# Reordering the seven first-layer products of a chunk: 1 2 6 5 7 1' 3 instead of 1 2 5 6 1' 3 7

## The chip, the cores and the metric

The kernel runs on one core of a Trainium2 chip. The metric is the device time of one launch in microseconds (us), the median of three runs. Engines are named as in the profile: PE is the matmul engine, PEld its weight loads, DVE the vector engine, ACT the scalar engine, POOL the GpSimd engine, SP the engine that issues most of the DMAs. Results of matmuls land in PSUM[...]; ACT and DVE read them from there.

## The reference

Two blocks follow each other. The first is an attention with a threshold, over 8 batches, 8 heads, 576 positions and a head width of 64, and the second a two-layer network on its output as 4608 tokens of width 512:

```python
def _attn_ref(q, k, v, tau) -> np.ndarray:
    scale = 1.0 / np.sqrt(q.shape[-1])
    scores = scale * np.matmul(q, k.transpose(0, 1, 3, 2))
    thresh = np.max(scores, axis=-1, keepdims=True) - tau
    scores = np.where(scores >= thresh, scores, -1000000000.0)
    scores = scores - np.max(scores, axis=-1, keepdims=True)
    attn = np.exp(scores)
    attn = attn / (np.sum(attn, axis=-1, keepdims=True) + 1e-09)
    return np.matmul(attn, v).astype(np.float32)

def _moe_ref(x, w_in, w_out) -> np.ndarray:
    h = x @ w_in
    r = np.maximum(h, 0.0)
    g = r * r
    return (g @ w_out).astype(np.float32)
```

`w_in` is 512 x 2048 and `w_out` 2048 x 512. All is in float32.

## The kernel before

The kernel interleaves the two blocks on one core. Attention runs in steps: a step takes 128 query rows of a pair of heads. The network runs in 18 chunks of 256 tokens, numbered 0 to 17. A chunk is cut into pieces (a handful of matmuls each), and the pieces are put between the attention's instructions as filler for PE: `fill` and `piece` take them from a queue in order, by a fixed count of microseconds per piece, not by a clock. So the place of each instruction in its engine's queue is set when the program is built[...].

**First layer of chunks 2 to 17.** These chunks compute x @ w_in as a 2 x 2 block product with seven block products instead of eight, on sums and differences of the blocks of x and of w_in. Each product comes in two halves of the hidden width; the first half is written "1", the second "1'". So there are 14 units, and `UNITS` gives their order. A unit (`unit`, line 678) is eight matmuls of 128 x 128 x 128 (line 693), 16 rows in the profile, since each float32 matmul shows as two. Its result needs a PSUM bank of 512 columns. The units build on each other in place:

- Product 1 takes a bank. Once it has been copied out, product 6 adds to the same bank; once 1+6 has been copied out, product 7 adds to it; once that has been read, product 4 adds.
- Product 5 takes a bank; once it has been copied out, product 3 adds to it.
- Product 2 takes a bank of its own.

In that stage the units have three banks (5, 6 and 7), so 1' takes the bank that product 2 leaves, and 2' the one that product 3 leaves.

**The readers of the banks.** After a unit, `then` (line 708) reads its bank into the buffer `g`: a copy on ACT for products 1 (line 713), 6 (line 718), 5 (line 725) and 7' (line 729), an add on DVE for 2, 3, 7, 2', 3' and 5' (line 705), and for 4 and 4' the activation itself. After an add, ACT runs the activation, Relu and Square (lines 701 and 702). `then` is issued one piece after its unit and the activation one piece after that (`after`, line 946), or earlier where an attention step calls `after` between pieces. On ACT these copies and activations stand in one queue with the attention's: two small ones (lines 340 and 341), two exponents (line 343) and a copy of one column (line 309) that makes ACT wait for the scores. On DVE the adds stand with the maxima of the scores (line 317), the threshold with its sum (line 355), the small lines 359 and 360, the turning of blocks (lines 459 to 469 and 254), and some sums of weight blocks (line 624).

**What else the units use.** The sums of token blocks T1, T2 (tile `t`), T3 (in place in `xT`) and T4 (in `held`) are made by POOL at line 670; unit 5 uses T1, 6 uses T2, 7 uses T3, 4 uses T4. The sums of weight blocks for 6, 5 and 3 are made at line 624, on POOL or, for 6' and 3', on DVE; they lie in `g`, in `gsum` and in `turned`, and some of them are made only when an earlier unit's `then` has asked for them.

**Around it.** The attention's scores are line 296 on PE, its values (weights times v) line 530, whose weights come by DMA through a store aside in DRAM (`aside`). POOL divides the weights (lines 365 and 367). The second layer (line 799) is again a seven-product form, in 14 pieces per chunk; its product 1 is put before the units 3' and 4'. The last three chunks run after the attention has ended, so nothing of it stands between their units.

The lines that carry the dependence on banks:

```python
        if p in "125":
            used[p, q] = keep_bank((p, q))
        to = used[{"6": "1", "7": "1", "4": "1", "3": "5"}.get(p, p), q].rearrange("p (f n) -> p f n", f=4)
```

## Time and profile before

| what | value |
|---|---|
| time, median of 3 runs | 1320.76 us (1320.71 to 1320.98) |
| the profiled execution's own time | 1320.85 us |
| its span in the profile | 1319.1 us |
| mean granted TensorE clock | 0.997 |
| line 693 (units), PE | 3584 rows, 272 to 377 ns each, median 275 |
| line 705 (adds), DVE | 96 of 680 ns median |
| line 713, copy of product 1 in chunk 6, ACT | 0.59 us |
| idle of DVE before line 705, waiting for line 693 | 78.1 us, 33 times |
| idle of ACT before line 713, waiting for line 693 | 39.7 us, 13 times |

A page of the profile shows one execution: the busy time of each engine, the span in 40 slices, the chain of work that ended last, and groups of instructions with the idle time of their engine before them. The timeline gives the instructions of a window in order, with start and length in us; instructions of one kind that follow each other are merged, so that "x32" at line 693 is two units. The arrow in brackets names what ended an engine's idle time. The ends of matmuls are modelled, so that a unit seems to end some 0.16 us after the next has begun.

### The profile page before, as it was taken

How to read it: one execution, taken by the hardware profiler on the slowest of the kernel's cores; microseconds unless marked ns; L12 is line 12 of the kernel's file. 1: busy time of each engine (PE TensorE's matmuls, PEld its weight loads, DVE VectorE, ACT ScalarE, POOL GpSimd, SP SyncE). 2: the span in 40 equal slices, each digit the busy share in tenths (PEclk: the TensorE clock that was granted, in tenths of full speed). 3: DMA queues.
4: the chain of work that ended last, by engine and by line, in shares of the span. 5: the costliest groups of instructions: out<-in, count | busy, mean ns of one | idle time of the engine just before them, and what ended most of it. 6: DMA issues, size and time to landing. Idle time of an engine off the chain costs nothing.

```text
span 1319.1 us, 24730 instructions
## 1 busy us (share of the span) xinstructions
PE 1290.9 (98%) x8862; PEld 1070.6 (81%) x8862; DVE 936.9 (71%) x2034; ACT 585.4 (44%) x1353; POOL 776.2 (59%) x908
## 2 busy tenths in 40 slices
PE   7999999999999999999999999999999999999997
PEld 6676557897888888797978888888887988889997
DVE  6899776777777788788776877878686877522131
ACT  4887763244343526253435343525353434331331
POOL 3788874775747475556574746656574737455351
PEclk9999999999999999999999999999999999999999
DMA  6765431777777878686666768667676866520000
GB/s 127 156 181 145 126 73 60 145 173 168 165 173 178 181 177 186 143 200 160 170 157 158 158 154 187 172 137 185 146 173 139 198 162 161 144 53 9 9 17 17
DMA packets 320907, 185.48 MB, mean 141 GB/s; under 512 B 282224, under 2 KB 282256, under 8 KB 314384
## 3 DMA queue, kind: packets, MB, share of 16 engines
q1 hardware_dynamic: 309120, 115.78, 46.4%
q0 software_dynamic: 10000, 67.92, 12.9%
q8 instruction: 70, 1.15, 0.4%
q14 instruction: 53, 0.43, 0.1%
q10 hardware_dynamic: 1664, 0.21, 0.1%
HBM read 108.04 MB, written 68.42 MB: 134 GB/s over the span
## 4 chain that ended last, share of the span: by engine, by line
PE 83%; DVE 6%; DMA 3%; ACT 2%; issue 1%; POOL 1%; SPq 0%; DVEq 0%; POOLq 0%; ACTq 0%
PE big L693 29%; PE big L799 28%; PE big L530 10%; PE big L296 8%; PE big L579 3%; PE big L764 2%; PE big L280 2%; DVE st L317 1%; DMA wT<-aside 1%; DMA aside<-turned 1%; PE big L414 1%; DVE w L355 1%; ACT w L343 1%; DVE turned L154 0%; PE big L273 0%
## 5 line engine op out<-in xcount | busy, mean ns | idle before, releaser
L355 DVE SCALAR_TENSOR_TENSOR w<-big,st,w 128x576 f32<-128x576 f32 x269 | 207.4, 805 | 87.6 <-ACT w L343 85.6
L317 DVE TENSOR_REDUCE st<-big 128x1 f32<-128x576 f32 x288 | 204.1, 747 | 85.3 <-PE big L296 60.6
L367 POOL TENSOR_SCALAR w<-w,st 128x576 f32<-128x576 f32 x269 | 244.2, 916 | 29.4 <-DVE st L360 24.6
L799 PE MATMUL big<-wo,gsum 128*128 128x256 f32 x1088 | 243.8, 382 | 0.0
L799 PEld LDWEIGHTS big<-wo,gsum 128*128 128x128 f32 x1088 | 204.4, 190 | 37.0 <-issue 7.6
L693 PE MATMUL big<-xT,w_in_sb 128*128 128x128 f32 x1536 | 187.4, 277 | 1.5 <-DVE g L705 1.4
L693 PEld LDWEIGHTS big<-xT,w_in_sb 128*128 128x128 f32 x1536 | 178.5, 192 | 10.8 <-issue 7.7
L799 PE MATMUL big<-wo,g 128*128 128x256 f32 x816 | 185.3, 382 | 0.1
L343 ACT ACTIVATE w<-big,st 128x576 f32<-128x576 f32 x255 | 174.4, 735 | 0.2 <-issue 0.2
L799 PEld LDWEIGHTS big<-wo,g 128*128 128x128 f32 x816 | 151.6, 190 | 26.2 <-issue 6.5
L530 PE MATMUL big<-wT,vs 128*64 128x256 f32 (+5 forms) x1420 | 159.5, 389 | 4.9 <-DMA wT<-aside 3.5
L530 PEld LDWEIGHTS big<-wT,vs 128*64 128x64 f32 (+1 forms) x1420 | 86.0, 136 | 70.1 <-issue 20.8
L340 ACT ACTIVATE st<-st 128x2 f32<-128x2 f32 (+1 forms) x137 | 28.1, 205 | 253.3 <-DVE st L317 252.1
L365 POOL TENSOR_SCALAR st<-st 128x2 f32<-128x2 f32 (+1 forms) x148 | 35.6, 241 | 177.7 <-DVE w L355 167.1
L436 POOL DMA_DIRECT2D aside<-turned x50 | 29.9, 597 | 177.5 <-DVE turned L465 177.5
L705 DVE TENSOR_TENSOR g<-big,g 128x512 f32<-128x512 f32 x96 | 64.6, 676 | 83.7 <-PE big L693 78.1
L296 PE MATMUL big<-kT,qT 64*128 64x256 f32 (+3 forms) x768 | 107.0, 416 | 0.0
L296 PEld LDWEIGHTS big<-kT,qT 64*128 64x128 f32 x768 | 84.6, 186 | 14.5 <-issue 5.0
L701 ACT ACTIVATE g<-g 128x512 f32<-128x512 f32 x96 | 60.4, 630 | 63.5 <-DVE g L705 63.4
L569 POOL TENSOR_TENSOR gsum<-g 128x512 f32<-128x512 f32 x34 | 46.1, 1356 | 69.9 <-ACT g L702 69.6
L702 ACT ACTIVATE g<-g 128x512 f32<-128x512 f32 x128 | 80.9, 632 | 4.0
L459 DVE STREAM_TRANSPOSE turned<-w 128x512 f32<-128x512 f32 x100 | 70.2, 702 | 0.3 <-issue 0.3
(119 smaller groups left out, 2058.1 us busy)
## 6 DMA issues: line engine op xcount, KB each, us to landing
aside<-turned POOLq DMA_DIRECT2D x50, 1152.0 KB, 4.8
wT<-aside SPq DMA_DIRECT2D x200, 288.0 KB, 5.4
vs<-in_v_dram SPq DMA_DIRECT2D x72, 128.0 KB, 5.7
wo<-in_moe_w_in_dram SPq DMA_DIRECT2D x16, 512.0 KB, 4.8
wo<-in_moe_w_out_dram SPq DMA_DIRECT2D x16, 512.0 KB, 3.5
out_dram<-osb POOLq DMA_DIRECT2D x32, 256.0 KB, 3.9
kl<-in_k_dram SPq DMA_DIRECT2D x113, 72.0 KB, 2.8
ql<-in_q_dram SPq DMA_DIRECT2D x112, 72.0 KB, 5.7
```

The lines of the kernel that those rows point to most:

```text
L296: nc.tensor.matmul(big[to, at + x0:at + x1], lhsT, keys[u * D:(u + 1) * D, x0:x1], start=True, stop=True)
L317: nc.vector.tensor_reduce(out=mx[:, u:u + 1], in_=sc[u], axis=AX.XY, op=ALU.max)
L343: nc.scalar.activation(out=w[:, u, :].rearrange("p (h k) -> p h k", h=2), in_=sc[u], func=AF.Exp, bias=bias[:, u:u + 1], scale=SCALE)
L355: nc.vector.scalar_tensor_tensor(out=wu, in0=sc[u], scalar=thr[:, u:u + 1], in1=wu, op0=ALU.is_ge, op1=ALU.mult, accum_out=sm[:, u:u + 1])
L367: nc.gpsimd.tensor_scalar(out=w[:, u, :], in0=w[:, u, :], scalar1=z[:, u:u + 1], scalar2=rcp[:, u:u + 1], op0=ALU.add, op1=ALU.mult)
L459: move(wb[:, 0:h, :, :], whole_[:, 0, :, :, :])
L530: nc.tensor.matmul(ps[u * D:(u + 1) * D, :], vs[n % 2][rows, u * (NBLK + 1) + c, :], wT[rows, at // REST:(at + ps.shape[1]) // REST, NBLK ...
L693: nc.tensor.matmul(to[:, f, :], factor(j, p, q, c)[:, f * P:(f + 1) * P], part[:, c, :], start=(p in "125" and f == 0 and c == 0), stop=(p ...
L701: nc.scalar.activation(out=to, in_=to if src is None else src, func=AF.Relu)
L702: nc.scalar.activation(out=to, in_=to, func=AF.Square)
L705: nc.vector.tensor_tensor(out=x, in0=to, in1=x, op=ALU.add)
L799: nc.tensor.matmul(to, left[:, f, :], wo[:, slot, f, :], start=(f == 0), stop=(f == HF - 1))
```

## The change

One string is changed, the order of the first twelve units. Products 6 and 5 change places, 7 moves from behind 3 to before 1', and 1' and 3 move back by one. From 6' on the order is as it was, and so are the two units that follow product 1 of the second layer.

```diff
-    UNITS = [(p[0], len(p) - 1) for p in "1 2 5 6 1' 3 7 6' 2' 4 7' 5'".split()], [("3", 1), ("4", 1)]
+    UNITS = [(p[0], len(p) - 1) for p in "1 2 6 5 7 1' 3 6' 2' 4 7' 5'".split()], [("3", 1), ("4", 1)]
```

The readers and requests that hang on a unit move with it: its copy or add, its activation, and the sums that its `then` asks for. It holds for chunks 2 to 17; chunks 0 and 1 don't use `UNITS`.

## The prediction

> **What bounds the kernel now.** I read the page first: its part on busy time, the 40 slices, then the chain that ended last.

> ```profile
> PE 1290.9 (98%) x8862; PEld 1070.6 (81%) x8862; DVE 936.9 (71%) x2034; ACT 585.4 (44%) x1353; POOL 776.2 (59%) x908
> ...
> PE   7999999999999999999999999999999999999997
> ...
> PE 83%; DVE 6%; DMA 3%; ACT 2%; issue 1%; POOL 1%; SPq 0%; DVEq 0%; POOLq 0%; ACTq 0%
> ```

> PE is busy 98% of the span, in every slice but the first and last at nine tenths or more, and the chain is PE for 83%. No other engine passes 71%. So a microsecond in which PE newly waits is a microsecond of time, and one that PE no longer waits comes off. What the other engines do counts only where PE waits for it.

> Next I asked for the instructions of line 693 (the units), and what ended PE's idle time before them:

> ```profile
>   issue: 12.9, 36
>   DVE g L705: 3.7, 6
>   POOL g L624: 1.7, 2
>   POOL gsum L624: 0.3, 1
>   POOL gsum L569: 0.3, 1
>   ACT g L718: 0.3, 1
> ```

> Real waits before 1,792 unit matmuls are 6.3 us in all (everything but "issue"). That is the most this stage can give back. The order of before costs nearly nothing, so what matters is whether the new order adds waits. The timeline of PE, ACT and DVE around chunk 6 (columns: start, length, engine, line, operation, operands, count, and idle time before it) shows how close the readers of the banks are:

> ```profile
> 558.32 3.84 PE L693 MATMUL big<-xT,w_in_sb 128*128 128x128 f32 x32
> ...
> 561.07 0.59 ACT L713 COPY g<-big 128x512 f32<-128x512 f32 x1
> ...
> 561.99 3.74 PE L693 MATMUL big<-t,g 128*128 128x128 f32 x32
> ...
> 564.75 0.68 DVE L705 TENSOR_TENSOR g<-big,g 128x512 f32<-128x512 f32 x1
> ...
> 565.46 0.63 ACT L701 ACTIVATE g<-g 128x512 f32<-128x512 f32 x1 [3.80 <-DVE g L705]
> 565.57 1.97 PE L693 MATMUL big<-xT,w_in_sb 128*128 128x128 f32 x16
> 566.12 0.63 ACT L702 ACTIVATE g<-g 128x512 f32<-128x512 f32 x1
> 566.66 0.57 ACT L725 COPY g<-big 128x512 f32<-128x512 f32 x1
> 567.13 0.59 ACT L718 COPY g<-big 128x512 f32<-128x512 f32 x1
> ```

> Units 1 and 2 run from 558.32, units 5 and 6 from 561.99, unit 1' from 565.57: a unit takes 1.79 us of PE. Unit 1's bank is copied at 561.07, unit 6's at 567.13, though unit 6 ended at 565.73: ACT stood at L701, which waited 3.80 us for DVE's add of unit 2. What a wait for a bank looks like is shown in chunk 12, where 1' takes the bank of unit 2 (read by DVE until 968.76):

> ```profile
> 968.82 2.05 PE L693 MATMUL big<-xT,w_in_sb 128*128 128x128 f32 x16 [0.96 <-DVE g L705]
> ```

> PE starts 0.06 us after the read ends, and this unit takes 1.89 instead of 1.79 us: 0.1 us a restart. The same 0.06 is in chunk 4 (423.38, 423.43).

> [...] the copy of unit 6 above stands behind L701. [...] the waits below stay under 2 us, so I cost no clock. The trace of before agrees in so far as its waits of 0.4 to 1 us at lines 530 and 693 left the granted clock at 9 tenths or more in every slice.

> **The change part by part.** Matmuls, copies, adds, squares and SP's DMAs are the same in number and size; SP's order is the same. The pieces keep their 14 places; only what stands in places 3 to 7 changes: 5 6 1' 3 7 becomes 6 5 7 1' 3. Banks stay: 1, 6, 7, 4 share one, 5 and 3 another, 1' takes that of 2, and 2' that of 3. The distances from a read to the unit that needs it done become:

> - 6 after the copy of 1 (L713): units between fall from two to one
> - 7 after the copy of 6 (L718): from two to one
> - 6' after the copy of 1': from two to one
> - 2' after the add of 3 (L705): from two to one
> - 3 after the copy of 5 (L725): two, as before
> - 1' after the add of 2: from two to three; 4 after the add of 7: from two to four

> One unit between leaves about 1.6 us from the end of the unit to the end of its read. With an empty ACT a copy ends 0.62 us after its unit (last three chunks of the trace), so these chunks, without attention beside them, lose nothing. In the others ACT's queue decides. In the new order of ACT's instructions the copy of 6 stands where that of 5 stood or earlier, so I take the time of the instruction in that slot from the timeline. Chunk by chunk, in us:

> - chunk 2: slot of copy 6 is that of L725, ended 282.69; unit 7 was due at 282.14: 0.61. Then 1' stands behind a group of scores (L296), and its copy behind that step's two exponents (L343, ended 288.95, now 0.6 later) and behind L701 and L702: 289.6+0.6+0.6+0.6=291.4; 6' was due at 290.5: 0.9. With two restarts 1.7.
> - chunk 5: L725's slot ended 495.33; place 5 began at 493.58: 1.8.
> - chunk 6: 567.23 against 565.57: 1.7, restart 0.1: 1.8.
> - chunk 8: 698.56 against 697.79: 0.8, restart 0.1: 0.9.
> - chunk 9: 767.07 against 765.87: 1.26 and 0.1. Unit 3 now stands behind the scores, and its add behind DVE's L317, L469, L355, L359, L360, which ended at 776.02 and come 1.4 later; with 0.65 for the add, 778.1; 2' is due at 776.7: 1.5 and 0.1. Together 2.95.
> - chunk 10: copy of 1 ended 827.41, unit 6 is due at 825.81: 1.66 and 0.1: 1.75.
> - chunk 11: copy of 1 ended 895.15, due 893.25: 1.96 and 0.1; unit 5's wait for POOL's L624 there (0.73 in the trace, its place 1.03 too long) goes: 1.0.
> - chunk 12: copy of 1 ended 965.70, due 964.04: 1.7 and 0.1; copy of 6 in the slot ending 970.56, so place 5 begins at 970.62 instead of 968.82, the wait of 1' included: 1.8 in all.
> - chunk 13: copy of 1' behind L355, L360 (ended 1042.2), add of 7, L701, L702: about 1044.7; 6' due at 1044.05: 0.75 and 0.1; a wait of 0.3 before 7' goes: 0.5.
> - chunk 4: the wait of 1' (0.44) goes, 3 waits for the copy of 5, which now stands behind the exponents (L718's slot, ended 426.89) as long: -0.1.
> - chunks 3, 7, 14: reads end 0.3 to 1 us early: nothing. Chunks 15 to 17: nothing.

> Sum: 1.7+1.8+1.8+0.9+2.95+1.75+1.0+1.8+0.5-0.1 = 14.1 us.

> Moved on DVE: the add of 7 now stands ahead of L317 or L355 of an attention step, so that step's maxima or threshold come up to 3 us later (chunk 8: unit 7 ends about 700.7, L317 began at 698.37). Behind them wait the exponents, POOL's division, the turning and the store aside. The steps' values are multiplied three or four steps later, so I cost nothing; without that cover L530 would wait, as it did for 3.5 us in all on DMA before. A later PE may shorten that 3.5: 0 to -2. Moved on POOL: in five chunks (3, 4, 10, 13, 14) the two sums for 5' (L624, 1.3 us each) go behind a division; chunk 4 is tightest, done at about 437 with 5' due at 438.4: nothing. T3 was done 10 us or more before its first use in most chunks and 5 us in chunk 15: nothing.

> The profiled execution took 1320.85 us, with 1319.1 of span and 1.75 around it; the median is 1320.76, so the two are one for this purpose. 1320.85+14.1 = 1335.0.

> **Rivals.**
> - Half of it: PE's delay and shifts in DVE's queue spare several of the waits, and only those from ACT's slots just behind exponents hold (5, 6, 10, 12: 7.2 us, less 2 for DMA waits): 1326. For it: DVE's L624 took 0.67 to 2.18 us, and the add of 2 behind it moves with it. Against: a unit and its copy shift together.
> - Cascade: the late adds on DVE and copies on ACT reach the tight places (chunks 4, 7, 11, 14, each with 0.1 to 1 us left) and L530's transfers: 8 us more, 1343.
> - Faster: the longer distances for 1' (add of 2), 4 and 5 remove the waits of the L693 view, of which 3.7 us are DVE's and 2.0 POOL's L624, while the copy of 6 gets ahead of L701 everywhere as it does in chunks 3, 4, 13 and 14. Then 1320.85-3 = 1318. It decides if the copies of 1 and 6 end within 1.6 us of their units; the slots above speak against it in eight chunks.
> - Nothing: gains and losses of 2 us each: 1320.8. It needs the same early copies.

> **How the numbers follow.** Forecast 0.70 (own range 1330 to 1340), half 0.14, cascade 0.09, faster 0.03, nothing 0.04. The range 1326 to 1342 leaves out the two last cases, half of the half and part of the cascade. A measurement of this kernel tells about 0.2%, 2.6 us, from no change: faster 0.03, same 0.05, slower 0.92.

> **What would show it.** Idle of PE before L693 ended by ACT's L713 and L718 should appear with some 10 to 12 us, by DVE's L705 some 1.5 to 3. In chunk 6 the fifth unit should start 1.7 us after the fourth ended. The last three chunks should be as long as before. PE's busy time should stay. If the L693 view shows no ACT release, the forecast is wrong; if L530 waits for DMA far more than 3.5 us, it is the cascade.

## The result and the profile after

| what | before | after |
|---|---|---|
| time, median of 4 runs each, same chip | 1320.74 us (1319.98 to 1320.98) | 1335.74 us (1333.27 to 1338.4) |
| ratio, 95% interval | | 1.0115 (1.0095 to 1.0135) |
| the profiled execution: time, span | 1320.85, 1319.1 us | 1335.76, 1334.0 us |

The new order costs 15 us. The page of after, its parts on busy time and on the chain that ended last:

```profile
PE 1294.1 (97%) x8862; PEld 1071.7 (80%) x8862; DVE 937.6 (70%) x2034; ACT 583.4 (44%) x1353; POOL 776.3 (58%) x908
...
PE 79%; DVE 8%; ACT 3%; DMA 3%; issue 2%; POOL 0%; SPq 0%; DVEq 0%; ACTq 0%; POOLq 0%
```

The counts of instructions are those of before, and PE is still what bounds the kernel. Its busy time grew by only 3.2 us, the span by 14.9: the rest is idle time of PE. What ended the idle time before line 693 (us, times; rows of PE and of weight loads together):

```profile
  issue: 14.0, 38
  ACT g L718: 13.7, 12
  ACT g L713: 7.7, 7
  POOL gsum L624: 3.9, 3
  DVE g L705: 2.5, 2
  POOL g L624: 2.0, 1
  ACT g L725: 0.6, 1
```

The two copies on ACT, 0.3 us in this view of before, now stand for 21.4. But this view counts a stall twice where the weight load and the matmul both wait. The view of waits, PE's own queue alone (total, times, longest), is the one to add up:

```profile
PE big L693 <- ACT g L718: 6.3, 6, 1.8
PE big L693 <- ACT g L713: 6.2, 5, 1.9
PE big L530 <- DMA wT<-aside: 3.3, 3, 1.4
PE big L693 <- DVE g L705: 1.1, 1, 1.1
PE big L693 <- ACT g L725: 0.6, 1, 0.6
```

PE waits 14.2 us at line 693, 12.5 of them for the copies of products 6 and 1. The same view of before had two lines for line 693, beside one for L530:

```profile
PE big L530 <- DMA wT<-aside: 3.5, 3, 1.6
...
PE big L693 <- DVE g L705: 1.4, 2, 1.0
...
PE big L693 <- POOL g L624: 0.7, 1, 0.7
```

The old waits of 1' (L705) and of unit 5 in chunk 11 (L624) went; the 1.1 us for L705 is a new one, of unit 2' in chunk 9. So 2.1 us went and 14.2 came in. L530's wait for its transfers did not change. One of the new waits, chunk 6, in the timeline of after (start, length, engine, line, operation, operands, count, idle time before it):

```profile
561.34 3.84 PE L693 MATMUL big<-xT,w_in_sb 128*128 128x128 f32 x32
...
564.09 0.59 ACT L713 COPY g<-big 128x512 f32<-128x512 f32 x1
...
565.02 3.74 PE L693 MATMUL big<-t,g 128*128 128x128 f32 x32
...
567.77 0.68 DVE L705 TENSOR_TENSOR g<-big,g 128x512 f32<-128x512 f32 x1
...
568.49 0.63 ACT L701 ACTIVATE g<-g 128x512 f32<-128x512 f32 x1 [3.81 <-DVE g L705]
569.15 0.63 ACT L702 ACTIVATE g<-g 128x512 f32<-128x512 f32 x1
569.68 0.57 ACT L718 COPY g<-big 128x512 f32<-128x512 f32 x1
...
570.30 2.94 PE L693 MATMUL big<-xT,w_in_sb 128*128 128x128 f32 x24 [1.55 <-ACT g L718]
```

Units 6 and 5 run from 565.02. Unit 6's bank was complete near 566.8, but its copy stands in ACT's queue behind L701, which waited 3.81 us for DVE's add of unit 2. The copy ended at 570.25 and unit 7 began 0.05 us later, 1.7 us behind its turn. Before, unit 1' stood in that place and needed another bank.

Laying the unit starts of the two traces side by side gives the delay that each chunk adds (us, from its first unit's start to its last unit's; under "where", by how much more the unit named starts late than the one ahead of it):

| chunk | predicted | measured | where |
|---|---|---|---|
| 2 | 1.7 | 1.45 | 7: 0.37, 6': 0.82 |
| 3, 7, 14 | 0 | 0 | |
| 4 | -0.1 | 0.35 | 7: -0.60, 3: 0.73, 6': 0.49 |
| 5 | 1.8 | 1.06 | 7: 1.80, 6': -0.67 |
| 6 | 1.8 | 1.72 | 7: 1.71 |
| 8 | 0.9 | 0.92 | 7: 0.82 |
| 9 | 2.95 | 2.76 | 7: 1.25, 2': 1.31 |
| 10 | 1.75 | 1.85 | 6: 1.74 |
| 11 | 1.0 | 2.70 | 6: 2.04, 5 and 7: 0.67 |
| 12 | 1.8 | 1.70 | 6: 1.80 |
| 13 | 0.5 | 0.38 | 6': 0.64, 7': -0.25 |
| 15 to 17 | 0 | 0 | |
| sum | 14.1 | 14.89 | last matmul of the trace: 14.91 later |

One chunk is off by more than 0.8 us, chunk 11. The timeline of PE there:

```profile
899.95 3.73 PE L693 MATMUL big<-xT,w_in_sb 128*128 128x128 f32 x32
...
905.56 5.44 PE L693 MATMUL big<-t,g 128*128 128x128 f32 x32 [1.88 <-ACT g L713]
```

After a gap of 1.88 us, two units take 5.44 us instead of 3.7. The stretches of this trace show why (start and end, length, busy time of PE, weight loads, DVE, ACT and POOL, granted clock, DMA share, GB/s):

```profile
902.60:906.00 3.40, 1.52 (x14) 1.36 (x13) 1.68 (x4) 2.13 (x5) 3.40 (x4) 1.00 0.70 159
906.00:909.40 3.40, 3.40 (x19) 3.40 (x18) 3.33 (x9) 1.72 (x3) 3.25 (x5) 0.50 1.07 204
909.40:912.80 3.40, 3.40 (x30) 3.16 (x29) 0.56 (x2) 0.77 (x3) 2.85 (x3) 1.00 1.24 252
```

The clock was 0.50 for one stretch of 3.41 us from 906.0: 19 rows of PE instead of 30.

### The profile page after: what moved, and what is told of

It is laid out like the page before. It is cut to its first block, busy times and chain, and to the rows that moved or that the text cites. A ratio compares the mean times of both kernels' runs of the same rounds, so it can differ in the third digit from the quotient of the medians.

```text
span 1334.0 us, 24740 instructions
## 1 busy us (share of the span) xinstructions
PE 1294.1 (97%) x8862; PEld 1071.7 (80%) x8862; DVE 937.6 (70%) x2034; ACT 583.4 (44%) x1353; POOL 776.3 (58%) x908
## 4 chain that ended last, share of the span: by engine, by line
PE 79%; DVE 8%; ACT 3%; DMA 3%; issue 2%; POOL 0%; SPq 0%; DVEq 0%; ACTq 0%; POOLq 0%
PE big L799 28%; PE big L693 25%; PE big L530 10%; PE big L296 8%; PE big L579 3%; DVE st L317 2%; PE big L764 2%; PE big L280 2%; DVE w L355 2%; DMA wT<-aside 1%; DMA aside<-turned 1%; ACT w L343 1%; PE big L414 1%; DVE turned L459 0%; DVE turned L154 0%
## 5 line engine op out<-in xcount | busy, mean ns | idle before, releaser
L317 DVE TENSOR_REDUCE st<-big 128x1 f32<-128x576 f32 x288 | 204.3, 748 | 97.0 <-PE big L296 70.7
L355 DVE SCALAR_TENSOR_TENSOR w<-big,st,w 128x576 f32<-128x576 f32 x269 | 207.8, 808 | 80.9 <-ACT w L343 78.6
L693 PE MATMUL big<-xT,w_in_sb 128*128 128x128 f32 x1536 | 185.1, 277 | 7.4 <-ACT g L718 6.3
L693 PEld LDWEIGHTS big<-xT,w_in_sb 128*128 128x128 f32 x1536 | 177.3, 192 | 16.5 <-ACT g L718 7.4
L343 ACT ACTIVATE w<-big,st 128x576 f32<-128x576 f32 x255 | 174.0, 732 | 0.2 <-issue 0.2
L530 PE MATMUL big<-wT,vs 128*64 128x320 f32 (+5 forms) x1420 | 159.7, 389 | 4.6 <-DMA wT<-aside 3.3
L530 PEld LDWEIGHTS big<-wT,vs 128*64 128x64 f32 (+1 forms) x1420 | 85.5, 136 | 70.6 <-issue 20.8
L705 DVE TENSOR_TENSOR g<-big,g 128x512 f32<-128x512 f32 x96 | 65.1, 678 | 92.7 <-PE big L693 87.1
L296 PE MATMUL big<-kT,qT 64*128 64x256 f32 (+3 forms) x768 | 106.5, 416 | 0.0
L296 PEld LDWEIGHTS big<-kT,qT 64*128 64x128 f32 x768 | 84.4, 186 | 14.3 <-issue 5.3
L569 POOL TENSOR_TENSOR gsum<-g 128x512 f32<-128x512 f32 x34 | 46.1, 1355 | 69.8 <-ACT g L702 63.9
L701 ACT ACTIVATE g<-g 128x512 f32<-128x512 f32 x96 | 60.3, 628 | 56.7 <-DVE g L705 56.6
L702 ACT ACTIVATE g<-g 128x512 f32<-128x512 f32 x128 | 80.7, 630 | 4.1
```

Of the source, the lines that this page charges most:

```text
L296: nc.tensor.matmul(big[to, at + x0:at + x1], lhsT, keys[u * D:(u + 1) * D, x0:x1], start=True, stop=True)
L317: nc.vector.tensor_reduce(out=mx[:, u:u + 1], in_=sc[u], axis=AX.XY, op=ALU.max)
L343: nc.scalar.activation(out=w[:, u, :].rearrange("p (h k) -> p h k", h=2), in_=sc[u], func=AF.Exp, bias=bias[:, u:u + 1], scale=SCALE)
L355: nc.vector.scalar_tensor_tensor(out=wu, in0=sc[u], scalar=thr[:, u:u + 1], in1=wu, op0=ALU.is_ge, op1=ALU.mult, accum_out=sm[:, u:u + 1])
L530: nc.tensor.matmul(ps[u * D:(u + 1) * D, :], vs[n % 2][rows, u * (NBLK + 1) + c, :], wT[rows, at // REST:(at + ps.shape[1]) // REST, NBLK ...
L693: nc.tensor.matmul(to[:, f, :], factor(j, p, q, c)[:, f * P:(f + 1) * P], part[:, c, :], start=(p in "125" and f == 0 and c == 0), stop=(p ...
```

## The experiments

Each was compared with runs of the kernel before on its own chip: median 1319.84 us for the first four, 1319.62 for the next four, and a single run of 1320.26 for the last two. Diffs are against the changed kernel, but for the control against the kernel before.

**Only 6 and 5 change places.**

```diff
-    ... "1 2 6 5 7 1' 3 6' 2' 4 7' 5'" ...
+    ... "1 2 6 5 1' 3 7 6' 2' 4 7' 5'" ...
```

> Order 1 2 6 5 1' 3 7 6': only 5 and 6 change places, 7 stays behind 3. Theory (a copy on ACT comes too late for the unit that adds to the same bank, because only one unit stands between): 6 still waits for the copy of 1 in chunks 10 to 12, 3 now has one unit between it and the copy of 5 and waits 0.4 to 1.6 us in chunks 3 to 6, 13 and 14; together 8 to 10 us, 1329 to 1331 us. Rival A (the add of 7, moved ahead of the attention's maxima and thresholds on DVE, delays the attention): DVE's order is that of before again, 1321 us.

Measured 1332.08 us, ratio 1.0092 (1.0071 to 1.0112). PE's waits:

```profile
PE big L693 <- ACT g L713: 5.1, 3, 1.9
PE big L530 <- DMA wT<-aside: 4.3, 3, 2.5
PE big L693 <- ACT g L725: 3.6, 4, 1.5
```

Unit 6 waits for the copy of 1 in chunks 10, 11 and 12 as in after (1.75, 2.04, 1.80). With 7 back in its old place the copy of 6 costs nothing, and 3 waits for the copy of 5 instead, which now has one unit between (chunks 3, 4, 5, 13, 14: 0.49 to 1.71). The time is 1 us above the range that was expected. The last matmul ends 11.9 us later. Two half-clock stretches are in that, one at chunk 11 and one at 554.8, behind a wait of L530 for its transfer that is 2.49 us long, 1.22 in before: ahead of chunk 6 the delay rises by 2.90.

**Only 7 moves forward.**

```diff
-    ... "1 2 6 5 7 1' 3 6' 2' 4 7' 5'" ...
+    ... "1 2 5 6 7 1' 3 6' 2' 4 7' 5'" ...
```

> Order 1 2 5 6 7 1' 3 6': only 7 moves, directly behind 6. Theory: no unit stands between 6 and 7, so 7 waits for the copy of 6 in nearly every chunk, also in the last three, where the copy alone (0.62 us after the unit) makes it 0.9 us each; from the ends of the copies of 6 in the trace of before I work out 27 us, and 3 us at 6' and 2': 1350 us. Rival A: the add of 7 stands on DVE as in the changed kernel, 1335 us.

Unit 7 here comes straight after 6. In chunks where nothing issues the copy in between, it stands behind unit 7 and takes in product 7 too, which changes that part of the computation. Measured 1349.75 us, ratio 1.0224 (1.0201 to 1.0247).

```profile
PE big L693 <- ACT g L718: 20.3, 8, 4.1
```

The total met the expectation, but by chance. The last three chunks lost nothing where 0.9 each was expected, for the reason just given. And some 11 us came from a source that was not expected: half-clock stretches at 355.1, 430.2 (two in a row), 580.4, 990.0, 1065.1 and 1136.8, each behind a gap of 2.0 us or more, which slow the units behind the gap. The two parts of the change don't add up, 12 and 30 against 15, nor do they without the half clocks in the traces, some 9 and 20 against 13: with 5 put between 6 and 7 the copy gets a unit's time, 1.79 us.

**Copies of 1 and 6 that don't read their banks.** They read a block of weights in place of the bank, so 6 and 7 need not wait for them, nor the copies for their own units; everything else, the order of ACT's queue included, stays.

```diff
-                nc.scalar.copy(g11, to)
+                nc.scalar.copy(g11, wo[:, Q00, 0:2, :].rearrange("p f (e n) -> p (f e) n", e=2))
...
-                nc.scalar.copy(g12, to)
+                nc.scalar.copy(g12, wo[:, Q00, 0:2, :].rearrange("p f (e n) -> p (f e) n", e=2))
```

> The changed kernel, but the copies of products 1 and 6 (both halves) read a constant block of the weights in SBUF instead of the bank, so that their result is left out of the output; ACT has the same copies in the same order. Theory: 6, 7 and 6' no longer wait for ACT, what stays is 2' in chunk 9 (1.4 us), 3 in chunk 4 (0.7) and the wait for POOL in chunk 11 (1 to 2): 1322 us, 1320 to 1325. Rival A and rival B (sums on POOL come too late): 1334 to 1336, since DVE's and POOL's orders are those of the changed kernel.

Measured 1319.06 us (12 runs), ratio 0.9997 (0.9989 to 1.0006). All of line 693's waits that are left:

```profile
PE big L693 <- DVE g L705: 1.1, 1, 1.1
PE big L693 <- ACT g L725: 0.4, 1, 0.4
```

The whole loss goes with these dependences, while the orders on DVE and POOL are those of after. The control, the same edit in the kernel before:

> The same in the kernel before: the copies of products 1 and 6 read a constant block. It is the control of the other one. All theories: nothing waits for these copies for more than 0.3 us there, so 1320 to 1321 us. If it is several us faster, the other run tells of the copies themselves and not of the order.

It measured 1320.28 us, ratio 1.0004 (0.9995 to 1.0013), so the edit by itself does nothing that can be told from noise. It also bounds what the order could ever give: with the copies at no cost in both, the new order is 1.2 us faster than the old one (medians of 12 runs each, on one chip), and in the two traces the delays of its chunks add up to 0.8 us less.

**One copy at a time.** The same edit on line 718 alone, then on 713 alone.

> The changed kernel, only the copies of product 6 (both halves) read a constant block instead of the bank and are left out of the result; the copies of 1 read their bank. Theory: the waits of 7 go; what stays is 6 behind the copy of 1 in chunks 10 to 12 (1.7, 2.0 and 0.6 net), 6' in chunks 2 and 13 (0.9, 0.4), 2' in chunk 9 (1.4), and 1.7 for the halved clock if the gap of 2 us in chunk 11 trips it again: 7 us over before, 1327 us where before is 1320. Rivals (DVE's order, POOL's order): 1334 or more.

> The changed kernel, only the copies of product 1 (both halves) read a constant block instead of the bank and are left out of the result; the copies of 6 read their bank. Theory: the waits of 6 and 6' go; 7 behind the copy of 6 stays in chunks 2, 5, 6, 8, 9 and 12 (0.5, 1.1 net, 1.7, 0.9, 1.3, 1.8 net), 2' in chunk 9 (1.4); no gap reaches 2 us, so the clock stays: 8.5 us over before, 1328.5 us where before is 1320. Rivals: 1334 or more.

With the copy of 6 made free, 1326.97 us, ratio 1.0054 (1.0038 to 1.0070). The total is as expected, though chunk 11's gap of 1.88 us was not followed by a half clock in this trace; in its stead 6' of chunk 6 came 0.99 us late, which was not expected. What the copies of 1 and 1' cost is then 1.0054 less the 0.9997 of both free, 0.0057 or 7.5 us. With the copy of 1 made free, 1328.38 us, ratio 1.0066 (1.0048 to 1.0083): by the same difference the copies of 6 and 6' cost 0.0069, 9.1 us. Their sum, 0.0126, is that of both together, 1.0115 less 0.9997 or 0.0118, within the intervals. In the second trace unit 7 of chunk 12 waits 2.83 us, which is 0.96 that 1' waited in its place before and 1.87 more, and a half clock follows (976.6), against the expectation that no gap reaches 2 us; in after unit 7 does not wait there, since 6 has waited already. So the same stall can be charged to either copy.

**The activations put off.** For 2 and 7 of the first half, lines 701 and 702 are put off so that the copies no longer stand behind them.

```diff
-            return [lambda: square(x)]
+            return [lambda: state["last"].append(lambda: square(x)) if p in "27" and not q else square(x)]
```

> The changed kernel, but Relu and Square of products 2 and 7 (first half) are issued one piece later, so that on ACT the copies of 6 and of 1' stand ahead of them. Nothing is left out. Theory: the copy of 6 no longer stands behind L701's wait for the add of 2, so 7's waits in chunks 5 and 6 (1.8 and 1.7 us) and nearly all in chunk 9 and 2 go; those of 6 in chunks 10 to 12, which come from the exponents, stay, and in chunks 3, 4 and 14 the copy of 5, now behind the squares, costs 3 about 0.5, 1.1 and 0.4 us: 9 us over before, 1329 us where before is 1320. Rivals: 1335, DVE's and POOL's orders are nearly the same.

Measured 1327.47 us, ratio 1.0058 (1.0040 to 1.0075). Chunk 6 in its timeline, PE, ACT and DVE:

```profile
564.68 0.58 ACT L718 COPY g<-big 128x512 f32<-128x512 f32 x1 [2.33 <-PE big L693]
565.46 0.68 DVE L705 TENSOR_TENSOR g<-big,g 128x512 f32<-128x512 f32 x1
...
566.17 0.63 ACT L701 ACTIVATE g<-g 128x512 f32<-128x512 f32 x1 [0.90 <-DVE g L705]
566.27 3.74 PE L693 MATMUL big<-xT,w_in_sb 128*128 128x128 f32 x32
```

The copy goes ahead of L701 and unit 7 starts without a wait, in chunks 2, 5 and 6, and with 0.07 us in chunk 9. That L701 ahead of it made the copy late is shown. The waits of 6 in chunks 10 to 12, whose copy stands behind the exponents, are as long as in after, and chunk 8's 0.82 stays; chunk 4's unit 3 is now 1.91 late. In this trace, too, chunk 11's gap of 1.88 us was not followed by a half clock.

**Filler in chunk 11's gap.** Eleven matmuls, transposes of a constant block, into a free bank, ahead of unit 6 of chunk 11.

```diff
+        (j, p, q) == (11, "6", 0) and keep_busy(11, next(b for b in oldest if b in (5, 6, 7) and b not in kept.values()))
```

> The changed kernel, with 11 transposes of a constant block before unit 6 of chunk 11, into a bank that unit 5 overwrites; they fill most of the 1.9 us in which PE waits there for the copy of 1. Theory of the clock: the gap of 2 us was what halved the granted clock for 3.4 us from 906.0, which cost 1.7 us; with PE busy it stays full there, places 3 to 5 of chunk 11 lose 1.0 us over before instead of 2.7, and the time is 1 to 2 us below the changed kernel's though PE has more to do. Rival: the halving has nothing to do with the gap: it stays, and the time is the changed kernel's or up to 0.4 us more.

Measured 1334.46 us, ratio 1.0114 (1.0097 to 1.0131), not to be told from after. In the trace there is no half clock at chunk 11, and its delay fell from 2.70 to 1.07:

```profile
906.36 1.36 PE L324 MATMUL big<-ident 128*128 128x128 f32 x11
908.40 3.81 PE L693 MATMUL big<-t,g 128*128 128x128 f32 x32 [0.67 <-ACT g L713]
```

But chunk 5, 1.06 in after, added 2.68:

```profile
492.96 3.74 PE L693 MATMUL big<-t,g 128*128 128x128 f32 x32
498.53 5.47 PE L693 MATMUL big<-xT,w_in_sb 128*128 128x128 f32 x32 [1.83 <-ACT g L718]
```

The gap there is the one that after has, of the same 1.83 us, and only here it was followed by a half clock. So the length of a gap alone does not decide. That led to the last two runs. The half-clock records of a run begin a whole number of 3.413 us after its first one; steps of this length, counted from that record, are called the grid of the run below.

**The changed kernel twice more, for its clock.**

> As the run before it, with its own grid: halved after chunk 11's gap only if a step begins between 902.1 and 903.8 (moved by as much as this run's chunk 11 is), after chunk 5's only if one begins between 493.9 and 495.5; nowhere else. The rival expects chunk 11 alone again.

They took 1335.16 and 1333.85 us. The first has a half-clock record at 905.5, a whole 260 steps after its first record; the second has none between its start and its end. Its chunk 11 in the timeline and in stretches of its grid:

```profile
899.66 3.73 PE L693 MATMUL big<-xT,w_in_sb 128*128 128x128 f32 x32
905.27 3.81 PE L693 MATMUL big<-t,g 128*128 128x128 f32 x32 [1.88 <-ACT g L713]
```

```profile
901.80:905.20 3.40, 1.59 (x15) 1.40 (x13) 1.67 (x3) 2.14 (x5) 3.40 (x4) 1.00 0.66 147
905.20:908.60 3.40, 3.33 (x30) 3.36 (x31) 3.33 (x9) 1.29 (x3) 3.35 (x5) 1.00 1.06 210
```

The same gap of 1.88 us, full clock after it, and a delay of 1.08 us in that chunk instead of 2.70. The rival, that the gap's length decides, has fallen. The grid theory did not fail, but this run is no sharp test of it: its step began at 901.8, just at the edge of where a halving was expected, with PE idle for 0.54 of it by the trace.

The run with filler is a sharper one. A step of its grid begins at 905.5, over chunk 11's gap. With the filler PE is idle for 0.20 of that step; without the filler's 1.36 us it would have been 0.55, the share that a half clock followed in after, in the swap of 6 and 5, and in the first repeat. So that filling the gap kept the clock, and not a lucky place of the grid, is what this trace points to.

## Why the prediction was right

**The mechanism is shown.** Taking away the dependence of 6 on the copy of 1, and of 7 on the copy of 6, takes away the loss, and each of the two carries about half of it. The distances in units, and ACT's queue as what decides, are as predicted: with L701 out of the way the copy of 6 is in time in chunks 2, 5, 6 and, to 0.07 us, 9.

**The slots.** Reading the end of a copy from the old instruction in the same place of ACT's queue was good to 0.25 us in the sums of chunks 2, 6, 8, 9, 10, 12 and 13, chunk 9's wait for DVE's add of 3 included. That the last three chunks lose nothing was right too.

**What hid the moved work held.** L530 waits 3.3 us for its transfers, 3.5 before. The cascade did not come. In the trace of the swap alone one such wait is 1.27 us longer than before; it is one trace, so it isn't shown that the order did that.

**The step that failed: "the waits below stay under 2 us, so I cost no clock".** The term of chunk 11, 1.0, was mis-sized: 2.70 in the first profile, of which 1.6 is the half clock; without it, in the third profile of the changed kernel (the last run), the chunk measured 1.08. That waits under 2 us cost no clock was the author's estimate, which the trace of before did not show: 1.88 us was enough here. What counted is how much of one step of 3.4133 us was idle, 0.55 of it in this case, as the last section works out, and not the length of the gap alone. The waits of before that the prediction leaned on, "0.4 to 1 us at lines 530 and 693", were misread as well: L530's in that trace are 0.69, 1.22 and 1.58 us. "PE's busy time should stay" failed with it: 3.2 us more in the first profile, 1.2 in the third (1292.1), which has no half clock between start and end.

**The sum came out close with two errors against each other.** Of the 14.89 us, 1.6 was clock that the sum did not have. The other terms together were 0.8 too high, most of it chunk 5, where the wait of 1.80 came but 0.67 of it was won back at 6', since the scores ahead of it (L296) took 2.21 us and not 2.88 as before. Chunk 4 was 0.45 too low: 3 was priced at the 0.44 that 1' no longer waits and came 0.73 late, and 6', priced at nothing, came 0.49 late, 0.42 of it because the scores ahead of it took 2.63 us and not 2.21. Why the scores took longer or shorter stays open. The forecast did not need the half clock to be near: in the third profile, which has none, the last matmul comes 13.0 us later than before.

**A view was misread.** "Real waits ... 6.3 us in all" added PE and weight loads, which wait for the same thing at once; on PE alone it was 2.1 us. So the faster rival's 3.7 and 2.0 us never existed as time. The kernel with free copies says what the longer distances are worth: 1.2 us against its control. (That its trace ends 1.2 us before that of before is another thing: the control's ends 1.4 us before it, and both lack the wait of 1.58 us at L530 that stands at 1162.1 in before.) The same slip touches "some 10 to 12 us" for the two copies: the view that it named shows 21.4, PE alone 12.5.

**The half rival** said that several waits would be spared. None of 0.8 us or more that was forecast for a copy in ACT's queue was spared; only one was partly won back.

## What to carry to other kernels

When work on one bank is put closer together, the price is the end of the reader in its own engine's queue, less the start of the next writer; take it from the instruction that holds that place in the queue today, and look at what stands ahead of it there. Add up the stalls on the engine's own queue only, since a view that also has the weight loads can count one twice: 21.4 us against 12.5 here. A stall of PE had a second price here, 1.6 us in chunk 11, where it left PE idle for 0.55 of a step of 3.4133 us. The same gap of 1.88 us left 0.29 to 0.55 of a step idle in the six profiles that have it unfilled, and a half clock followed in three of them, so its price changed from run to run.

## What the runs showed of the clock

In all twelve profiles half-clock records start a whole number of 3.4133 us after the first of their run, to 0.001 of a step (they last one step, or two in a row; only the last record of a run, at the program's end, had another length, 5.97 us in before and 3.33 in after). The phase against the kernel's start differs: the first record was at 16.8 to 18.9 us. Laying each run's grid over PE's busy time, between 50 and 1310 us:

| share of the step in which PE was idle | steps | followed by a half clock |
|---|---|---|
| 0.55 to 0.83 | 11 | 11 |
| 0.52 to 0.54 | 12 | 3 |
| below 0.50 | all others | 1 |

The one below 0.50 is 0.41, in the step of the "only 7" kernel that was itself at half clock. So in these profiles a half clock followed each step with 0.55 or more, and some of those with 0.52 to 0.54; the ends of matmuls are modelled, so these shares aren't known to better than a few hundredths. The kernel before doesn't exceed 0.36 on its grid between 60 and 1306 us, nor 0.47 wherever the grid were laid, and its trace has no half clock between 21.5 and 1315.1 us; in after, the gaps ahead of unit 7 in chunk 5 and of unit 6 in chunk 11 reach 0.53 and 0.55, in about half of the phases each. The gap of 1.88 us stands unfilled in six of the twelve profiles: a half clock followed in three, where it made 0.55 of a step, and none in the other three, where the step with the most of it had 0.29, 0.53 and 0.54. How often it comes over many runs wasn't tried.
